# The last chunk of a batch as 128 partitions of seven rows and 64 of one, instead of 120 of eight

## The chip, the core and the metric

The kernel runs on one NeuronCore of a Trainium2 chip. A core has five engines that run side by side: TensorE (PE; its weight loads are shown as PEld), VectorE (DVE), ScalarE (ACT), GpSimd (POOL) and SyncE (SP), which here issues every DMA. The DMAs run on 16 DMA engines. On-chip tiles have up to 128 partitions. The metric is the time of one execution on the device in microseconds; lower is better.

## The reference

Four batches of attention over columns, then a soft mixture of experts over all 20,224 rows of the result:

```python
B, N, C = (4, 5056, 256)
qn = q / (np.linalg.norm(q, axis=1, keepdims=True) + 1e-06)
kn = k / (np.linalg.norm(k, axis=1, keepdims=True) + 1e-06)
s = kn.transpose(0, 2, 1) @ qn / tau          # 256 x 256 a batch, summed over N rows
a = softmax(s)                                # over the last axis
x = (v @ a).reshape(B * N, C)
logits = x @ phi                              # 32 slots
d = softmax(logits, axis=0)                   # over all 20,224 rows
slot_input = d.T @ x
slot_out[e] = np.maximum(slot_input[e] @ w1[e], 0) @ w2[e]     # 8 experts, 4 slots each
c = softmax(logits, axis=1)
out = c @ slot_out
```

All data are float32.

## The kernel before

The 5,056 rows of a batch are cut into chunks of 1,024 rows. In a chunk each of the 128 partitions holds eight rows (J = 8) that follow each other in memory, 1 KB a row. Four chunks take 4,096 rows; 960 are left, and the fifth and last chunk is laid out as 120 partitions of eight:

```python
while t0 < N:
    pc = min(P, (N - t0) // J)
    chunks.append((t0, pc))
    t0 += pc * J
```

Everything that touches a chunk works on `:pc` partitions, so on 120 of them for the last chunk of each batch. Rows may stand on any partition, as the sums over rows don't depend on their order, and the softmax over slots is by row; only the store has to put each row back in its place.

**Scores.** `load_qk` loads q and k in halves of four rows a partition into a tile `raw` (five buffers; L135 for q, L136 for k: 512 KB each, 480 KB in the last chunk). `scores_chunk` makes a rounded copy and a remainder of some of the rows (`hl`: the cast on ScalarE, L160; the difference on VectorE, L161), squares for the norms (ScalarE, L164; added up on VectorE, L188 to L194), and the scores `S` on TensorE (L179). `attention` (L202 to L267) turns the scores of a batch into a matrix M; it takes a power on GpSimd (L218).

**Slots.** `load_v` loads v chunk by chunk (six buffers, L144). `turn_v` transposes a chunk on TensorE (`vTp`, L288) and copies it out (`vT`, L295 and L293). `logits_chunk` makes the logits `L` (L313): the 1,024 columns of a chunk stand as four groups of 32 partitions, and where the last chunk has fewer, a memset fills in −1e30 (L309). `gather_chunk` sums weighted rows of v into `G` (L401), after which the buffer of that v chunk is free.

**Experts and output.** The weights come as 1 MB tiles (L551, L554). At the end, for each chunk, TensorE forms the output from `soh` and `sol` (L733, L734), ScalarE and VectorE copy it out of PSUM (L737, L739) into a tile `o`, and a DMA stores it (L746, L748: 1 MB a chunk, 960 KB for the last of a batch).

**Order.** The order of SP's DMAs is that of the program text: the loads of q and k run ahead, v chunks between them. Each of them waits for its buffer to be free, and for one of eight semaphores that the DMAs take in turn, so that at most eight are on their way. What waits on SP holds up all DMAs behind it. On the other engines a scheduler sets the order up to the last batch; from there TensorE's order too is that of the text. Each engine then works through its order in turn.

Of the kernel before, what the change touches and what calls it, by code (L numbers as in the profile page):

```python
# [17 lines left out]
def colnorm_attention_soft_moe(  # L18
# [29 lines left out]
    PRE = 2  # L48
    NF = F // P
    HF = 4  # L50
    chunks = []
    t0 = 0
    while t0 < N:
        pc = min(P, (N - t0) // J)
        chunks.append((t0, pc))
        t0 += pc * J
    NCH = len(chunks)
    NT = NCH * J

    const = ctx.enter_context(tc.tile_pool(name="const", bufs=1))  # L60
# [47 lines left out]
    mend = keep.tile([P, 1], F32, name="mend")  # L108
    groups = [[(0, 3), (3, NCH)]] * B

    def rows(t, b, ch):
        t0, pc = chunks[ch]
        return t[b, t0 : t0 + pc * J, :].rearrange("(p j) c -> p j c", j=J)

    NS = 3

# [5 lines left out]
    ctx.enter_context(tc.manual_schedule(engines={mybir.EngineType.SP}))  # L122
    st = [dict() for _ in range(B)]

    def half_rows(t, b, ch, h):
        t0, pc = chunks[ch]
        t0 += h * pc * HJ
        return t[b, t0 : t0 + pc * HJ, :].rearrange("(p j) c -> p j c", j=HJ)

    def load_qk(b, ch):  # L130
        pc = chunks[ch][1]
        r = []
        for h in range(2):
            raw = apool.tile([P, 2, HJ, C], F32, tag="raw", name=f"raw{b}_{ch}_{h}", bufs=5)
            nc.sync.dma_start(raw[:pc, 0], half_rows(q, b, ch, h))  # L135
            nc.sync.dma_start(raw[:pc, 1], half_rows(k, b, ch, h))  # L136
            r.append(raw)
        st[b]["raw", ch] = r

    def load_v(b, ch, vt=None):  # L140
        pc = chunks[ch][1]
        if vt is None:
            vt = vpool.tile([P, J, C], F32, tag="v", name=f"v{b}_{ch}")
        nc.sync.dma_start(vt[:pc], rows(v, b, ch))  # L144
        st[b]["v", ch] = vt

    def scores_chunk(b, ch):
# [150 lines left out]
    def logits_chunk(b, ch):  # L298
        pc = chunks[ch][1]
        M = st[b]["M"]  # L300
        lo, hi = [g for g in groups[b] if g[0] <= ch < g[1]][0]
        if ch == lo:
            st[b]["mx", lo] = bpool.tile([P, 3], F32, tag="mxs", name=f"mxs{b}_{ch}", bufs=2)
            st[b]["lt", lo] = bpool.tile([P, 3, J, S], F32, tag="lt", name=f"lt{b}_{ch}", bufs=2)
        lt, mxs = st[b]["lt", lo], st[b]["mx", lo]
        L = pb.tile([P, 2, J, S], F32, tag="amisc" if b == B - 1 and ch == NCH - 2 else "L", name=f"L{b}_{ch}")[:, 0]
        rem = pc - S * (G - 1)
        if rem < S:
            nc.vector.memset(L[S * (G - 1) :, :, rem:], -1e30)  # L309
        for m in range(2):  # L310
            for g in range(G):
                w = min(S, pc - S * g)
                nc.tensor.matmul(  # L313
                    L[S * g : S * g + S, :, :w],
                    M[:, m, :],
                    st[b]["vT", ch, m][:, :, S * g : S * g + w],
                    start=m == 0,
                    stop=m == 1,
                )
# [391 lines left out]
    for b in range(B):  # L711
        for ch in range(NCH):
# [26 lines left out]
                    ev = nc.vector.tensor_copy(od, op[:pc])  # L739
            if (b, ch) in CE:  # L740
                combine(CE[b, ch], ev, nc.vector)
            r0 = b * N + t0
            dst = out[r0 : r0 + pc * J, :].rearrange("(p j) c -> p j c", j=J)
            if b == 0 and ch == 0:
                for lo, hi in CUT:
                    nc.sync.dma_start(dst[:, lo:hi, :], ot[:pc, lo:hi])  # L746
            else:
                nc.sync.dma_start(dst, ot[:pc])  # L748


_INS = ["q", "k", "v", "tau", "moe_phi", "moe_w1", "moe_w2"]
# [36 lines left out]
```

## Time and profile before

| | |
|---|---|
| median of 3 runs | 344.69 us (343.5 to 347.13) |
| profiled execution | 342.7 us, of which the profile's span is 340.9 |
| mean granted TensorE clock | 0.971 |
| busy: TensorE / weight loads / VectorE / ScalarE / GpSimd | 90% / 70% / 73% / 70% / 3% |
| DMA | 100.04 MB, mean 293 GB/s; read 78.94 MB, written 20.71 MB |
| chain that ended last | TensorE 53%, DMA 13%, VectorE 13%, ScalarE 10% |

The rows of the profile name an engine, a line of the kernel, an operation, and what it writes and reads. A shape such as `120*128` after a matmul gives the rows and columns of TensorE that it uses. "x4" is a count. What stands in brackets, or behind the bar, is how long the engine had been idle just before, and what ended it. "DMA to landing" is the time from the issue of a DMA on SP until all of it has arrived. In the stretches "DMA share" is how busy the 16 DMA engines were, and PEclk the share of TensorE's full clock that was granted.

### The profile page before, as it was taken

The page shows a single profiled execution, that of the slowest core. Times are in us where ns is not written, and L with a number is a line of the kernel's source. Part 1 is how long each engine was busy: PE and PEld are TensorE (multiplying, and loading weights), DVE is VectorE, ACT ScalarE, POOL GpSimd, SP SyncE. Part 2 cuts the span into 40 slices and gives each one's busy share as a digit, 9 for nine tenths or more (in the row PEclk, how much of TensorE's full clock was granted, in tenths as well). Part 3 has the DMA queues.
Part 4 walks back from the last instruction along what each step waited for, and adds up shares of the span by engine and source line. Part 5 has one row for each costly group of instructions (what it writes and reads, how often), then busy time and mean ns, then how long its engine had stood idle before and what let it go on. Part 6 is the DMA issues. An engine that isn't in the chain of part 4 may idle for free.

```text
span 340.9 us, 6200 instructions
## 1 busy us (share of the span) xinstructions
PE 305.3 (90%) x2460; PEld 239.9 (70%) x2460; DVE 250.3 (73%) x410; ACT 237.3 (70%) x306; POOL 11.5 (3%) x16
## 2 busy tenths in 40 slices
PE   3999899979999998999999899998889998989850
PEld 2898788979788877877887675665544575767530
DVE  1788999986789894978799397578968077986440
ACT  3788889966998975889799395554334258795620
POOL 0000001000001000000100000105000000000000
PEclk9999999998999998799999999999999999999995
DMA  6999989998797179999903994999979317999995
GB/s 252 380 388 255 398 304 374 299 316 315 248 324 258 52 214 275 418 370 288 375 14 101 271 318 121 423 294 417 413 272 426 127 60 320 310 412 360 373 404 196
DMA packets 20244, 100.04 MB, mean 293 GB/s; under 512 B 2744, under 2 KB 2744, under 8 KB 13240
## 3 DMA queue, kind: packets, MB, share of 16 engines
q1 hardware_dynamic: 20216, 99.66, 81.9%
q8 instruction: 19, 0.31, 0.4%
q14 instruction: 9, 0.07, 0.1%
HBM read 78.94 MB, written 20.71 MB: 292 GB/s over the span
## 4 chain that ended last, share of the span: by engine, by line
PE 53%; DMA 13%; DVE 13%; ACT 10%; issue 5%; SPq 2%; POOL 0%; DVEq 0%; ACTq 0%
PE S L179 18%; DMA raw<-in_k_dram 8%; PE vTp L288 7%; DMA v<-in_v_dram 5%; PE op L733 5%; PE L L313 4%; ACT sq L164 4%; PE op L734 4%; PE G L401 3%; ACT hl L160 2%; DVE o L739 2%; PE H L648 2%; PE O L674 2%; PE cTp L722 2%; DVE sq L188 1%
## 5 line engine op out<-in xcount | busy, mean ns | idle before, releaser
L179 PE MATMUL S<-hl 128*128 128x256 f32 (+1 forms) x648 | 102.0, 304 | 0.8 <-ACT hl L160 0.4
L179 PEld LDWEIGHTS S<-hl 128*128 128x128 f32 (+1 forms) x648 | 86.5, 197 | 8.6 <-issue 4.1
L164 ACT ACTIVATE sq<-raw 128x2048 f32<-128x2048 f32 (+1 forms) x40 | 76.9, 1922 | 10.7 <-DVE sq L188 4.7
L161 DVE TENSOR_TENSOR hl<-raw,hl 128x1536 fp32r<-128x1536 f32 (+3 forms) x39 | 63.5, 1628 | 18.3 <-ACT hl L160 18.2
L160 ACT CAST hl<-raw 128x1536 fp32r<-128x1536 f32 (+3 forms) x39 | 53.8, 1380 | 21.8 <-DMA raw<-in_k_dram 12.0
L179 PE MATMUL S<-raw 128*128 128x256 f32 (+1 forms) x208 | 55.9, 403 | 9.5 <-DMA raw<-in_k_dram 7.8
L188 DVE TENSOR_TENSOR sq<-sq,sq 128x2048 f32<-128x2048 f32 (+1 forms) x20 | 45.8, 2288 | 7.7 <-ACT sq L164 7.3
L179 PEld LDWEIGHTS S<-raw 128*128 128x128 f32 (+1 forms) x208 | 39.3, 204 | 14.5 <-issue 8.2
L288 PE MATMUL vTp<-ident,v 128*128 128x128 f32 (+1 forms) x320 | 42.7, 275 | 3.0 <-DMA v<-in_v_dram 2.9
L295 ACT COPY vT<-vTp 128x512 f32<-128x512 f32 (+1 forms) x70 | 39.2, 589 | 8.2 <-PE vTp L288 7.3
L288 PEld LDWEIGHTS vTp<-ident,v 128*128 128x128 f32 (+1 forms) x320 | 35.3, 142 | 9.5 <-issue 6.8
L733 PE MATMUL op<-soh,cT 128*128 128x512 f32 (+1 forms) x80 | 34.1, 426 | 4.5 <-ACT o L737 2.3
L737 ACT COPY o<-op 128x1024 f32<-128x1024 f32 (+1 forms) x26 | 26.4, 1023 | 10.1 <-PE op L734 10.1
L734 PE MATMUL op<-sol,cT 128*128 128x512 f32 (+1 forms) x80 | 31.6, 395 | 0.0
L739 DVE COPY o<-op 128x1024 f32<-128x1024 f32 (+1 forms) x14 | 17.1, 1223 | 13.0 <-PE op L734 13.0
L313 PE MATMUL L<-vT,M 128*32 128x256 f32 (+1 forms) x320 | 22.8, 383 | 1.7 <-DVE cm L570 1.5
L189 DVE TENSOR_TENSOR sq<-sq 128x1024 f32<-128x1024 f32 (+1 forms) x20 | 24.3, 1213 | 0.0
L733 PEld LDWEIGHTS op<-soh,cT 128*128 128x128 f32 (+1 forms) x80 | 14.9, 186 | 12.7 <-DVE o L739 5.7
L401 PE MATMUL G<-v,dn 128*32 128x256 f32 (+1 forms) x320 | 20.0, 382 | 0.5 <-DVE zacc L389 0.5
L727 ACT CAST cT<-cTp 128x512 fp32r<-128x512 f32 (+1 forms) x20 | 11.7, 589 | 10.3 <-PE cTp L722 5.3
L734 PEld LDWEIGHTS op<-sol,cT 128*128 128x128 f32 (+1 forms) x80 | 15.0, 187 | 2.4
L401 PEld LDWEIGHTS G<-v,dn 128*32 128x32 f32 (+1 forms) x320 | 9.8, 109 | 7.0 <-ACT gs L430 1.0
(122 smaller groups left out, 285.4 us busy)
## 6 DMA issues: line engine op xcount, KB each, us to landing
raw<-in_q_dram SPq DMA_DIRECT2D x32, 512.0 KB, 7.4
raw<-in_k_dram SPq DMA_DIRECT2D x32, 512.0 KB, 8.1
v<-in_v_dram SPq DMA_DIRECT2D x16, 1024.0 KB, 8.7
w<-in_moe_w_dram SPq DMA_DIRECT2D x16, 1024.0 KB, 15.7
out_dram<-o SPq DMA_DIRECT2D x15, 1024.0 KB, 6.6
raw<-in_q_dram SPq DMA_DIRECT2D x8, 480.0 KB, 8.4
raw<-in_k_dram SPq DMA_DIRECT2D x8, 480.0 KB, 10.1
v<-in_v_dram SPq DMA_DIRECT2D x4, 960.0 KB, 15.6
```

The lines of the kernel that those rows point to most:

```text
L160: nc.scalar.copy(hl[:pc, 0, :, :ns], raw[:pc, :, :ns])
L161: nc.vector.tensor_tensor(hl[:pc, 1, :, :ns], raw[:pc, :, :ns], hl[:pc, 0, :, :ns].bitcast(F32), op=ALU.subtract)
L164: nc.scalar.activation(sq[:pc], raw[:pc], AF.Square)
L179: nc.tensor.matmul(sps[:, m, :], lhs, rhs, start=first and y == 0 and m == 0, stop=last and y == len(pairs) - 1, skip_group_check=True,)
L188: nc.vector.tensor_tensor(s0[:pc], s0[:pc], s1[:pc], op=ALU.add)
L288: nc.tensor.transpose(tp[:, jj, :pc], vt[:pc, 4 * hh + jj, P * m : P * m + P], ident[:pc, :pc])
L295: nc.scalar.copy(dst, tp[:, :, :pc])
L313: nc.tensor.matmul(L[S * g : S * g + S, :, :w], M[:, m, :], st[b]["vT", ch, m][:, :, S * g : S * g + w], start=m == 0, stop=m == 1,)
L401: nc.tensor.matmul(gp[S * g : S * g + S, :], dn[ch - lo][:pc, j, :], vt[:pc, j, :], start=ch == lo and j < G, stop=ch == hi - 1 and j >= G,)
L733: nc.tensor.matmul(dst, cT[:, 2 * hh + jj, :pc], soh, start=True, stop=False)
L734: nc.tensor.matmul(dst, cT[:, 2 * hh + jj, :pc], sol, start=False, stop=True)
L737: nc.scalar.copy(od, op[:pc])
```

## The change

The last chunk now uses all 128 partitions. Its 960 rows are 128 partitions of seven rows (896 rows) and 64 partitions that have one row more; the eighth row of the other 64 partitions (`TL` = 64 and up) doesn't exist. A generator `pieces` yields, for each load or store of a chunk, one part or, where the eighth row is in it, two. So for the last chunk the second halves of q and k are two DMAs each (128 partitions of 3 KB, 64 of 1 KB), v is two (128 of 7 KB, 64 of 1 KB), and the store is two. That is 16 DMAs more. The missing eighth row is filled with zeros in q, k and v by memsets on GpSimd, and with −1e30 in the logits by VectorE. All other operations on the last chunk work on 128 partitions, or on 256 and 224 columns in the logits where they had three times 256 and once 192.

```diff
-    chunks = []
-    t0 = 0
-    while t0 < N:
-        pc = min(P, (N - t0) // J)
-        chunks.append((t0, pc))
-        t0 += pc * J
-    NCH = len(chunks)
+    NCH = -(-N // (P * J))
+    chunks = [(P * J * ch, P) for ch in range(NCH)]
+    JL = (N - chunks[-1][0]) // P
+    TL = N - chunks[-1][0] - P * JL
...
+    def pieces(rows, ch, j0, j1):
+        t0 = chunks[ch][0]
+        jm = min(j1, JL) if ch == NCH - 1 else j1
+        lo = t0 + P * j0
+        yield slice(0, P), slice(j0, jm), rows[lo : lo + P * (jm - j0), :].rearrange("(p j) c -> p j c", j=jm - j0)
+        if jm < j1:
+            lo = t0 + P * JL
+            yield slice(0, TL), slice(JL, J), rows[lo : lo + TL, :].rearrange("(p j) c -> p j c", j=1)
...
     def load_qk(b, ch):
-        pc = chunks[ch][1]
         r = []
         for h in range(2):
             raw = apool.tile([P, 2, HJ, C], F32, tag="raw", name=f"raw{b}_{ch}_{h}", bufs=5)
-            nc.sync.dma_start(raw[:pc, 0], half_rows(q, b, ch, h))
-            nc.sync.dma_start(raw[:pc, 1], half_rows(k, b, ch, h))
+            if ch == NCH - 1 and h == 1:
+                nc.gpsimd.memset(raw[TL:, :, HJ - 1, :], 0.0)
+            for x, t in enumerate((q, k)):
+                for ps, js, src in pieces(t[b], ch, HJ * h, HJ * h + HJ):
+                    nc.sync.dma_start(raw[ps, x, js.start - HJ * h : js.stop - HJ * h, :], src)
             r.append(raw)
...
-        nc.sync.dma_start(vt[:pc], rows(v, b, ch))
+        if ch == NCH - 1:
+            nc.gpsimd.memset(vt[TL:, JL, :], 0.0)
+        for ps, js, src in pieces(v[b], ch, 0, J):
+            nc.sync.dma_start(vt[ps, js, :], src)
...
-        rem = pc - S * (G - 1)
-        if rem < S:
-            nc.vector.memset(L[S * (G - 1) :, :, rem:], -1e30)
+        if ch == NCH - 1:
+            nc.vector.memset(L[TL:, JL, :], -1e30)
         for m in range(2):
             for g in range(G):
-                w = min(S, pc - S * g)
+                je = JL if ch == NCH - 1 and S * g >= TL else J
                 nc.tensor.matmul(
-                    L[S * g : S * g + S, :, :w],
+                    L[S * g : S * g + S, :je, :],
                     M[:, m, :],
-                    st[b]["vT", ch, m][:, :, S * g : S * g + w],
+                    st[b]["vT", ch, m][:, :je, S * g : S * g + S],
...
-            r0 = b * N + t0
-            dst = out[r0 : r0 + pc * J, :].rearrange("(p j) c -> p j c", j=J)
...
             else:
-                nc.sync.dma_start(dst, ot[:pc])
+                for ps, js, dst in pieces(out[b * N : b * N + N, :], ch, 0, J):
+                    nc.sync.dma_start(dst, ot[ps, js, :])
```

Lines after the new function stand two or three further down than before (L179 is now L182, L401 is L403, L748 is L750).

On SP, at the loads of the last chunk of batch 2 (`raw_4_0` and `raw_4_1` are its two halves, `v_1` and `v_2` chunks of batch 1), before:

```order
L144 DMA v_1_220<-in_v_dram 128x2048
L135 DMA raw_4_0_222<-in_q_dram 120x1024
L136 DMA raw_4_0_222<-in_k_dram 120x1024
L135 DMA raw_4_1_225<-in_q_dram 120x1024
L136 DMA raw_4_1_225<-in_k_dram 120x1024
L144 DMA v_2_228<-in_v_dram 128x2048
```

and now:

```order
L147 DMA v_1_228<-in_v_dram 128x2048
L136 DMA raw_4_0_230<-in_q_dram 128x1024
L136 DMA raw_4_0_230<-in_k_dram 128x1024
L136 DMA raw_4_1_233<-in_q_dram 128x768
L136 DMA raw_4_1_233<-in_q_dram 64x256
L136 DMA raw_4_1_233<-in_k_dram 128x768
L136 DMA raw_4_1_233<-in_k_dram 64x256
L147 DMA v_2_239<-in_v_dram 128x2048
```

The first half is one DMA for q and one for k, as before, but of 128 partitions; the second is two for each. The order of the tiles is the same.

On POOL, from the first power (`rn`, one for each batch) on, the number behind a tile's name being its batch, before:

```order
L218 TENSOR_TENSOR rn0_504<-rn0_504,half_88 128x4
L218 TENSOR_TENSOR rn1_902<-rn1_902,half_88 128x4
L218 TENSOR_TENSOR rn2_1508<-rn2_1508,half_88 128x4
L700 MEMSET sol_2913 128x512
L218 TENSOR_TENSOR rn3_2243<-rn3_2243,half_88 128x4
```

and now:

```order
L133 MEMSET raw0_4_1_151 64x2x256
L221 TENSOR_TENSOR rn0_520<-rn0_520,half_88 128x4
L133 MEMSET raw1_4_1_188 64x2x256
L145 MEMSET v0_4_210 64x256
L221 TENSOR_TENSOR rn1_918<-rn1_918,half_88 128x4
L133 MEMSET raw2_4_1_233 64x2x256
L145 MEMSET v1_4_256 64x256
L221 TENSOR_TENSOR rn2_1524<-rn2_1524,half_88 128x4
L133 MEMSET raw3_4_1_279 64x2x256
L145 MEMSET v2_4_2192 64x256
L145 MEMSET v3_4_2204 64x256
```

Behind these follow the memset of `sol` and the power of batch 3, as before. Each power now has one to three memsets ahead of it, which wait until the buffer that they fill is free.

On TensorE, among the scores of batch 3 (`S`, here of its chunk 3) stand the gathers `G_0` of batch 1, whose end frees the v buffers that SP waits for ahead of the last chunk's halves; before:

```order
L288 MATMUL vTp_0_1_1_1941<-ident,v_0_253 128x128 x4
L179 MATMUL S_1630<-hl_3_0_1962 128x256 x4
L401 MATMUL G_0_1603<-v_0_212,dn_0_1597 32x256 x8
L401 MATMUL G_0_1603<-v_1_220,dn_0_1597 32x256 x8
L401 MATMUL G_0_1603<-v_2_228,dn_0_1597 32x256 x8
```

and now:

```order
L291 MATMUL vTp_0_1_1_1957<-ident,v_0_266 128x128 x4
L182 MATMUL S_1646<-raw_3_0_268 128x256 x2
L182 MATMUL S_1646<-hl_3_0_1978 128x256 x11
L403 MATMUL G_0_1619<-v_0_220,dn_0_1613 32x256 x3
L254 MATMUL aTp_1547<-ident,a_1537 128x128 x2
L403 MATMUL G_0_1619<-v_0_220,dn_0_1613 32x256
L254 MATMUL aTp_1547<-ident,a_1537 128x128 x2
L403 MATMUL G_0_1619<-v_0_220,dn_0_1613 32x256 x4
L403 MATMUL G_0_1619<-v_1_228,dn_0_1613 32x256 x8
L403 MATMUL G_0_1619<-v_2_239,dn_0_1613 32x256 x8
```

The gathers moved behind more of the scores and between the transposes `aTp`; the count of TensorE that SP waits for is 1046 for the first of the v chunks, and was 1035. The same gathers in batch 2 have moved by less: the count there is 641, and was 642.

More of the change, by code (lines that the diff above doesn't have):

```diff
@@ L50, in colnorm_attention_soft_moe @@
     HF = 4
-    chunks = []
-    t0 = 0
-    while t0 < N:
-        pc = min(P, (N - t0) // J)
-        chunks.append((t0, pc))
-        t0 += pc * J
-    NCH = len(chunks)
+    NCH = -(-N // (P * J))
+    chunks = [(P * J * ch, P) for ch in range(NCH)]
+    JL = (N - chunks[-1][0]) // P
+    TL = N - chunks[-1][0] - P * JL
+    assert JL == J - 1 and TL % S == 0 and 0 < TL < P
     NT = NCH * J
@@ L109, in colnorm_attention_soft_moe @@
     groups = [[(0, 3), (3, NCH)]] * B
-    def rows(t, b, ch):
-        t0, pc = chunks[ch]
-        return t[b, t0 : t0 + pc * J, :].rearrange("(p j) c -> p j c", j=J)
+    def pieces(rows, ch, j0, j1):
[6 more added lines that the diff above has]
+            yield slice(0, TL), slice(JL, J), rows[lo : lo + TL, :].rearrange("(p j) c -> p j c", j=1)
     NS = 3
@@ L123, in colnorm_attention_soft_moe @@
     st = [dict() for _ in range(B)]
[L125 to L128, printed above, removed]
     def load_qk(b, ch):
-        pc = chunks[ch][1]
         r = []
@@ L741, in colnorm_attention_soft_moe @@
                 combine(CE[b, ch], ev, nc.vector)
-            r0 = b * N + t0
-            dst = out[r0 : r0 + pc * J, :].rearrange("(p j) c -> p j c", j=J)
             if b == 0 and ch == 0:
+                dst = out[: P * J, :].rearrange("(p j) c -> p j c", j=J)
                 for lo, hi in CUT:
-                    nc.sync.dma_start(dst[:, lo:hi, :], ot[:pc, lo:hi])
+                    nc.sync.dma_start(dst[:, lo:hi, :], ot[:, lo:hi])
             else:
-                nc.sync.dma_start(dst, ot[:pc])
+                for ps, js, dst in pieces(out[b * N : b * N + N, :], ch, 0, J):
+                    nc.sync.dma_start(dst, ot[ps, js, :])
 _INS = ["q", "k", "v", "tau", "moe_phi", "moe_w1", "moe_w2"]
```

## The prediction

> **What bounds the kernel now.** I read the page first, then the stretches, then the rows where TensorE stands still.
>
> ```profile
> span 340.9 us, 6200 instructions
> ...
> PEclk9999999998999998799999999999999999999995
> ...
> PE 53%; DMA 13%; DVE 13%; ACT 10%; issue 5%; SPq 2%; POOL 0%; DVEq 0%; ACTq 0%
> PE S L179 18%; DMA raw<-in_k_dram 8%; PE vTp L288 7%; DMA v<-in_v_dram 5%; PE op L733 5%; PE L L313 4%; ACT sq L164 4%; PE op L734 4%; PE G L401 3%; ACT hl L160 2%; DVE o L739 2%; PE H L648 2%; PE O L674 2%; PE cTp L722 2%; DVE sq L188 1%
> ```
>
> The chain that ended last is TensorE work for 53%; for 13% it is a wait for loads of k and v. The clock row is nearly all nines, with an 8 and a 7 inside the run. So TensorE is the bound, and what can be won there is the time in which it waits for a load, and the half clock that follows. Whether the changed transfers are behind this, the stretches tell:
>
> ```profile
> core 0: us, PE busy (x) PEld busy (x) DVE busy (x) ACT busy (x) POOL busy (x), PEclk, DMA share, GB/s
> 14.10:24.30 10.20, 10.20 (x68) 9.56 (x67) 9.29 (x9) 8.33 (x7) 0.00 (x0) 1.00 1.03 412
> 26.20:34.80 8.60, 8.26 (x54) 7.50 (x54) 7.75 (x7) 6.78 (x5) 0.00 (x0) 1.00 1.01 264
> 75.50:78.90 3.40, 3.40 (x17) 3.22 (x16) 0.00 (x0) 0.63 (x1) 0.00 (x0) 0.50 0.94 359
> 133.50:140.30 6.80, 6.68 (x27) 5.99 (x27) 6.80 (x9) 6.38 (x8) 0.00 (x0) 0.50 0.98 379
> 326.30:333.70 7.40, 2.78 (x11) 1.56 (x9) 2.45 (x2) 1.07 (x2) 0.00 (x0) 0.85 1.01 421
> ```
>
> In the first stretch only q and k halves of 128 partitions land, in the second mainly those of 120 partitions (batch 0, last chunk). The DMA engines are full in both (share 1.0), but move 412 GB/s in one and 264 in the other. A half of 512 KB (524,288 bytes) thus costs 524,288 / 412,000 = 1.27 us of the queue, a 120-partition half of 480 KB 491,520 / 264,000 = 1.86 us, though it is smaller. The same in batch 2, seen at its landings:
>
> ```profile
> 120.82 0.33 SPq L144 DMA_DIRECT2D v<-in_v_dram  x1
> 121.25 0.39 SPq L135 DMA_DIRECT2D raw<-in_q_dram  x1
> 121.69 0.40 SPq L136 DMA_DIRECT2D raw<-in_k_dram  x1
> ```
>
> ```profile
> v<-in_v_dram SPq DMA_DIRECT2D x1, 1024.0 KB, 4.9
> raw<-in_q_dram SPq DMA_DIRECT2D x2, 480.0 KB, 9.1
> raw<-in_k_dram SPq DMA_DIRECT2D x2, 480.0 KB, 11.3
> ```
>
> The v chunk lands at 120.82 + 4.9 = 125.7. Where TensorE waits, below, the first k half of 120 partitions has just landed, at 131.5: two such halves took 5.8 us, 2.9 each. I take 1.86 and 2.9 as the bounds of one, and 2.2 as the value, nearer the stretch, in which the queue is never empty.
>
> ```profile
> 64.55 9.74 DMA v<-in_v_dram
> ```
>
> ```profile
> 74.42 0.63 PE L288 MATMUL vTp<-ident,v 128*128 128x128 f32 x4 [2.16 <-DMA v<-in_v_dram]
> ...
> 131.62 1.10 PE L179 MATMUL S<-raw 120*128 120x256 f32 x4 [1.17 <-DMA raw<-in_k_dram]
> ...
> 194.65 1.10 PE L179 MATMUL S<-raw 120*128 120x256 f32 x4 [1.18 <-DMA raw<-in_k_dram]
> 196.14 0.38 PE L179 MATMUL S<-hl 120*128 120x256 f32 x1 [0.39 <-ACT hl L160]
> ```
>
> These are TensorE's longest waits for loads after the start: site A at 74.4 (a v chunk queued behind batch 1's four 120-partition halves), B at 131.6 and C at 194.7 (the 120-partition halves of batches 2 and 3 themselves). A and B stand just ahead of the two stretches at clock 0.50, C is followed by none.
>
> **The change, part by part.** Sums are against the profiled execution, 342.7 us (span 340.9, 1.8 around it); the median of the runs is 344.69, 2.0 more, and I add that at the end.
>
> *Loads.* Per batch, four slow halves (4 × 2.2 = 8.8 us of queue) become two full halves (2 × 1.27), two of 384 KB (393,216 / 412,000 = 0.95) and two pieces of 64 KB. A 64-row transfer is not in the trace. Its bytes alone are 0.16 us; from above it is bounded by what a whole small transfer takes from issue to landing:
>
> ```profile
> out_dram<-o SPq DMA_DIRECT2D x2, 256.0 KB, 2.3
> out_dram<-o SPq DMA_DIRECT2D x1, 512.0 KB, 2.9
> ```
>
> From 256 to 512 KB only 0.6 us are added, so most of the 2.3 is latency, which a full queue overlaps. Nearest is the issue time of a row above, 0.4 us, the pace at which SP can hand such pieces over; I take 0.4, and keep 0.16 and 2.3. New queue time: 2.54 + 1.9 + 0.8 = 5.2 us a batch against 8.8, so 3.6 earlier behind the chunk (2.2 if a slow half is only 1.86), and at B the first k half lands at 125.7 + 2 × 1.27 = 128.3, not 131.5.
>
> - Site A: v needs to be 74.3 − 72.3 = 2.0 us earlier, and comes 3.6 earlier. The wait of 2.16 goes, and with it, if the clock follows the wait, the half clock: 3.4 us full of matmuls at 0.50 lose about 1.6. Gain 3.7. What is late next is ScalarE's cast (L160), which itself waited for TensorE there.
> - Site B: k is there at 128.3, before TensorE arrives at 130.45 (131.62 − 1.17). Gain 1.17, plus up to half of 6.68 us of matmuls at 0.50; I take 3.0. Gain 4.2.
> - Site C: the waits are 1.18 + 0.39 = 1.6. But the rows moved here: the gather matmuls of batch 1 stand further back among the scores of batch 3, and SP, which waits for them before it issues a v chunk and behind it the last halves of batch 3, waits for a count of TensorE that is 11 higher. Eleven score matmuls are
>
> ```profile
> 186.20 1.55 PE L179 MATMUL S<-hl 128*128 128x256 f32 x11
> ```
>
> 1.5 us. The first k half comes 2 × (1.86 − 1.27) = 1.2 to 3.3 us sooner behind its v chunk, and that chunk 1.5 later: they about cancel. Gain 0.1, between −0.3 and 1.6.
> - Batch 0: VectorE and ScalarE carry the chain there; I count nothing.
>
> [...]
>
> *Stores.* In the last part VectorE paces the chunks:
>
> ```profile
> 327.04 1.24 DVE o L739
> ...
> 329.62 1.23 DVE o L739
> ```
>
> 2.58 us each; the queue moves a full chunk at 421 GB/s in 1,048,576 / 421,000 = 2.49. Queue and pace nearly match, so each slow store leaves a backlog:
>
> ```profile
> out_dram<-o SPq DMA_DIRECT2D x3, 1024.0 KB, 3.9
> ```
>
> ```profile
> out_dram<-o SPq DMA_DIRECT2D x1, 960.0 KB, 9.0
> ```
>
> The first three full stores land 3.9 us after their issue, the last store, the kernel's end, 9.0 after. With two parts (917,504 / 421,000 = 2.18, and 0.4) a batch's five chunks take 4 × 2.49 + 2.6 = 12.6 us of queue against 12.9 us of pace: no backlog grows. The last store then lands 3.9 + 0.4 (second issue) = 4.3 after: gain 4.7, I take 4.5. With 2.3 for the piece, 14.4 against 12.9 leaves 1.5 a batch, and the gain is gone.
>
> *Added work.* Transposes of v see 128 columns for 120:
>
> ```profile
> L288 PE MATMUL vTp<-ident,v 128*128 128x128 f32 x256 | 34.6, 276 | 3.0 <-DMA v<-in_v_dram 2.9
> ...
> L288 PE MATMUL vTp<-ident,v 120*128 120x120 f32 x64 | 8.3, 270 | 0.0
> ```
>
> 64 × 6 ns = 0.4 us, on the bound. The logits keep their columns (two of 256 and two of 224, for three of 256 and one of 192). The eight memsets on POOL are each at most
>
> ```profile
> L699 POOL MEMSET soh<- 128x512 f32 x1 | 0.5, 524 | 6.4 <-DVE vT L293 6.4
> ...
> POOL rn L218 <- DVE rn L217: 161.2, 3, 54.9
> ```
>
> 0.5 us, and are covered: POOL sits idle for 161 us in three stretches ahead of the power (L218) that every batch's softmax needs. They stand ahead of that power in POOL's order, but wait for readers of buffers that SP also waits for before the same chunk's load, long before the power. If that cover failed, softmax and all behind it would wait. The casts and first scores of the last half now wait for memset and load; the load is longer. Sixteen more issues at 0.4 us on SP fall where SP waits for buffers anyway.
>
> Sum: 3.7 + 4.2 + 0.1 + 4.5 − 0.4 = 12.1; 342.7 − 12.1 = 330.6, and 2.0 to the median: **332.6 us**.
>
> **Rivals.**
> 1. *Only the end is won.* TensorE's waits at A and B are taken over by casts and by SP, which waits for the gathers before it loads, and the half clock shows up elsewhere. For it: ScalarE and VectorE are busy for most of these stages; the clock's dips are two events in one execution. Against it: at B both were idle for the load. It gives 342.7 − 4.5 + 0.4 = 338.6, 340.6 at the median's level.
> 2. *The transfers don't get faster:* the low rate comes from the place in memory or from what runs beside. Against it: loads and stores of 120 partitions both are slow, full chunks ahead and behind aren't. It gives 344.7 ± 1. [...]
> 3. *Slower: the pieces of 64 rows are full-price transfers.* If one takes over (8.8 − 4.4) / 2 = 2.2 us of the queue, the last chunk lands later than now, and that decides. At the 2.3 of the 256 KB row it is about break-even. At the 2.9 of the 512 KB row the halves are 2 × 0.7 = 1.4 us later, at A, B and C together 4.2, less the 1.2 that the first k half still wins at B; the stores leave 4 × 2.49 + 2.18 + 2.9 − 12.9 = 2.1 a batch, 8.6 in all, where they leave 9.0 − 3.9 = 5.1 now, 3.5 more. That is 342.7 + 3.0 + 3.5 + 0.4 = 349.6, with 2.0 351.6. Against it: halves that follow each other land at 1.27 us, so a transfer's own latency is not paid in the queue. [...]
>
> **How the numbers follow.** Forecast (327 to 336) 0.62, the first rival (337 to 341) 0.18, the second 0.12, the third 0.08. The low end takes C in full (1.6), B's full half clock (3.4) and the slow halves at 2.9: 327.5. The range goes from there through the first rival, which leaves out some 0.2: **327.5 to 341**. About 1% (3.4 us) is what a measurement here can tell from no change: faster, below 341.2, gets the forecast and most of the first rival, 0.79; same 0.14; slower 0.07.
>
> **What would show it.** Right: the stretches in which batches 0 to 3 load their last chunks move about 400 GB/s; TensorE's row at the first v transpose of chunk 2 (A) and at the last halves (B, C) has no wait for a load; the clock row has nines where the 8 and the 7 stood; the last store lands some 4 us after its issue. Wrong: transfers of 64 rows that land 2 us or more behind their neighbours, a power on POOL that starts behind a memset, or half-clock stretches of 3.4 us that only moved.

## The result, and the profile after

| | before | changed |
|---|---|---|
| median, same chip | 345.91 us (4 runs, 343.5 to 348.1) | 333.12 us (4 runs, 331.1 to 336.4) |
| ratio | 1 | 0.961, 95% interval 0.951 to 0.972 |
| profiled execution, span | 342.7, 340.9 us | 331.1, 328.9 us |
| mean granted clock | 0.971 | 0.987 |

The change saves 12.8 us in the medians, 11.6 in the profiled executions. The ratios, here and below, leave out as slow each run that is over 1.5% above the fastest of its kernel; the medians hold all runs. The page after, in the lines that stood first in the prediction:

```profile
span 328.9 us, 6253 instructions
...
PEclk9999999999999999999999999999997999999997
...
PE 60%; DVE 13%; ACT 11%; issue 6%; DMA 6%; SPq 1%; POOL 1%; DVEq 0%; ACTq 0%; POOLq 0%
PE S L182 20%; PE vTp L291 8%; PE op L735 5%; ACT sq L167 5%; PE G L403 4%; PE L L315 4%; PE op L736 4%; DMA raw<-in_k_dram 4%; PE H L650 3%; DVE o L741 2%; PE O L676 2%; PE cTp L724 2%; DMA v<-in_v_dram 2%; DVE sq L191 2%; ACT hl L163 2%
```

The chain waits for loads of k and v for 6% where it was 13%. The two 8s and the 7 inside the clock row are gone, but a 7 has come at slice 31, among the experts. The stretches, the first with 128-partition halves as before, the next two in which the last chunks of batches 2 and 3 land:

```profile
core 0: us, PE busy (x) PEld busy (x) DVE busy (x) ACT busy (x) POOL busy (x), PEclk, DMA share, GB/s
14.10:24.30 10.20, 10.16 (x66) 9.24 (x65) 9.30 (x9) 8.39 (x7) 0.52 (x1) 1.00 1.03 412
...
122.70:129.70 7.00, 7.00 (x52) 6.05 (x50) 3.77 (x7) 5.28 (x4) 0.00 (x0) 1.00 1.04 375
184.20:189.80 5.60, 5.60 (x52) 4.52 (x51) 4.87 (x5) 3.02 (x3) 0.00 (x0) 1.00 1.05 374
```

A last chunk now loads at about 375 GB/s, and TensorE is busy for every microsecond of both stretches. TensorE's rows at the three sites (the bracket is the wait and what ended it):

```profile
72.96 0.63 PE L291 MATMUL vTp<-ident,v 128*128 128x128 f32 x4 [1.01 <-DMA v<-in_v_dram]
...
127.77 1.03 PE L182 MATMUL S<-raw 128*128 128x256 f32 x4
...
188.23 1.03 PE L182 MATMUL S<-raw 128*128 128x256 f32 x4
```

The first half of the last chunk has no bracket any more at B and C. A still has one, of 1.01 us. The last store of the program, its two parts and the time from issue to landing:

```profile
out_dram<-o SPq DMA_DIRECT2D x1, 896.0 KB, 3.8
out_dram<-o SPq DMA_DIRECT2D x1, 64.0 KB, 3.6
```

That was 9.0. Cut at the starts of the four copies of the finished scores on ScalarE (`ssb<-S`, L213, L210 before) and at the last copy of `o`, two traces of the changed kernel (the second is an experiment below) stand against before like this, in us:

| stretch | before | changed | changed, again |
|---|---|---|---|
| scores of batch 0 | 41.8 | 42.3 | 42.4 |
| batch 1 (site A) | 45.8 | 42.7 | 44.2 |
| batch 2 (site B) | 57.2 | 53.0 | 53.1 |
| batch 3 (site C) | 61.7 | 60.2 | 61.9 |
| from there to the last copy of `o` | 123.1 | 124.4 | 122.7 |
| from there to the last landing | 11.3 | 6.3 | 6.3 |
| span | 340.9 | 328.9 | 330.6 |

Two rows repeat to 0.1 us: site B (−4.1) and the end (−5.0). Sites A and C and the experts differ by 1.5 to 1.7 us between two executions of the same program, so one trace doesn't size them.

### The profile page after: what moved, and what is told of

It is laid out like the page before. It is cut to its first block, busy times and chain, and to the rows that moved or that the text cites. A ratio compares the mean times of both kernels' runs of the same rounds, so it can differ in the third digit from the quotient of the medians.

```text
span 328.9 us, 6253 instructions
## 1 busy us (share of the span) xinstructions
PE 302.8 (92%) x2460; PEld 236.5 (72%) x2460; DVE 249.7 (76%) x410; ACT 237.1 (72%) x306; POOL 14.7 (4%) x24
## 4 chain that ended last, share of the span: by engine, by line
PE 60%; DVE 13%; ACT 11%; issue 6%; DMA 6%; SPq 1%; POOL 1%; DVEq 0%; ACTq 0%; POOLq 0%
PE S L182 20%; PE vTp L291 8%; PE op L735 5%; ACT sq L167 5%; PE G L403 4%; PE L L315 4%; PE op L736 4%; DMA raw<-in_k_dram 4%; PE H L650 3%; DVE o L741 2%; PE O L676 2%; PE cTp L724 2%; DMA v<-in_v_dram 2%; DVE sq L191 2%; ACT hl L163 2%
## 5 line engine op out<-in xcount | busy, mean ns | idle before, releaser
L182 PE MATMUL S<-hl 128*128 128x256 f32 x648 | 98.9, 298 | 0.7 <-DVE hl L164 0.7
L182 PEld LDWEIGHTS S<-hl 128*128 128x128 f32 x648 | 83.7, 190 | 8.3 <-issue 4.5
L167 ACT ACTIVATE sq<-raw 128x2048 f32<-128x2048 f32 x40 | 77.0, 1924 | 11.2 <-DVE sq L191 6.0
L164 DVE TENSOR_TENSOR hl<-raw,hl 128x1536 fp32r<-128x1536 f32 (+1 forms) x39 | 63.5, 1627 | 8.0 <-ACT hl L163 8.0
L163 ACT CAST hl<-raw 128x1536 fp32r<-128x1536 f32 (+1 forms) x39 | 53.9, 1382 | 14.0 <-DMA raw<-in_k_dram 8.5
L182 PE MATMUL S<-raw 128*128 128x256 f32 x208 | 53.9, 392 | 7.3 <-DMA raw<-in_k_dram 5.7
L191 DVE TENSOR_TENSOR sq<-sq,sq 128x2048 f32<-128x2048 f32 x20 | 45.8, 2288 | 7.3 <-ACT sq L167 7.1
L182 PEld LDWEIGHTS S<-raw 128*128 128x128 f32 x208 | 38.0, 197 | 11.6 <-issue 5.6
L291 PE MATMUL vTp<-ident,v 128*128 128x128 f32 x320 | 43.5, 277 | 1.8 <-DMA v<-in_v_dram 1.0
L298 ACT COPY vT<-vTp 128x512 f32<-128x512 f32 x70 | 39.2, 597 | 6.1 <-PE vTp L291 5.5
L735 PEld LDWEIGHTS op<-soh,cT 128*128 128x128 f32 x80 | 15.0, 187 | 12.5 <-DVE o L741 5.6
L403 PE MATMUL G<-v,dn 128*32 128x256 f32 x320 | 20.8, 382 | 0.5 <-DVE zacc L391 0.5
L403 PEld LDWEIGHTS G<-v,dn 128*32 128x32 f32 x320 | 9.9, 109 | 7.1 <-ACT gs L432 1.0
```

Source lines behind the costliest of these rows:

```text
L163: nc.scalar.copy(hl[:pc, 0, :, :ns], raw[:pc, :, :ns])
L164: nc.vector.tensor_tensor(hl[:pc, 1, :, :ns], raw[:pc, :, :ns], hl[:pc, 0, :, :ns].bitcast(F32), op=ALU.subtract)
L167: nc.scalar.activation(sq[:pc], raw[:pc], AF.Square)
L182: nc.tensor.matmul(sps[:, m, :], lhs, rhs, start=first and y == 0 and m == 0, stop=last and y == len(pairs) - 1, skip_group_check=True,)
L191: nc.vector.tensor_tensor(s0[:pc], s0[:pc], s1[:pc], op=ALU.add)
L291: nc.tensor.transpose(tp[:, jj, :pc], vt[:pc, 4 * hh + jj, P * m : P * m + P], ident[:pc, :pc])
```

## The experiments

The kernels were timed on three chips, on each beside the kernel before. Two of the ratios' bases are thin: that of q and k only rests on two of its six runs, and on the third chip (the last three rows) before scattered from 337.6 to 350.9 us and only three of its twelve runs count. So the ratio of the medians stands beside, and kernels on the third chip are compared by their medians.

| kernel | median us (runs) | before, same chip | ratio, 95% | of medians |
|---|---|---|---|---|
| q and k only | 341.35 (6) | 343.76 | 0.975, 0.967 to 0.983 | 0.993 |
| v and stores only | 339.21 (6) | 343.76 | 0.989, 0.984 to 0.995 | 0.987 |
| old stores | 337.10 (6) | 343.76 | 0.979, 0.973 to 0.986 | 0.981 |
| old q, k in batch 2 | 334.78 (6) | 346.25 | 0.965, 0.958 to 0.971 | 0.967 |
| pieces in four | 331.97 (6) | 346.25 | 0.960, 0.955 to 0.966 | 0.959 |
| v ahead | 333.88 (6) | 346.25 | 0.965, 0.960 to 0.971 | 0.964 |
| old q, k in batch 1 | 334.90 (6) | 344.34 | 0.984, 0.977 to 0.992 | 0.973 |
| old q, k in batch 3 | 335.76 (6) | 344.34 | 0.987, 0.979 to 0.996 | 0.975 |
| changed, again | 332.53 (6) | 344.34 | 0.979, 0.971 to 0.987 | 0.966 |

### Transfers by themselves

Only DMAs, in groups: `dma_start(t[:rows, :j], q[...])`, eight back to back into eight buffers (four at 8 KB a row), for several numbers of rows and of KB a row.

> Transfers alone: the attention and the experts are left out, and what is stored is a constant. Groups of eight loads back to back (four in the groups with 8 KB a partition), each group started after the one before has landed: 128, 120, 112, 96 and 64 partitions of 4 KB, 124 and 60 partitions of 4 KB, 128 of 3 KB, 128 of 3 KB and 64 of 1 KB in turn, 64 of 1 KB alone, 128 and 120 of 8 KB; then four stores each of 128 and of 120 partitions of 8 KB, and of 128 of 7 KB with 64 of 1 KB. My theory, a 120-partition transfer is slow by its shape: 128x4 KB at about 410 GB/s (1.27 us each), 120x4 KB at about 264 (1.86 us each), stores of 120x8 KB slower by the same factor than 128x8 KB, and a 64-row piece adds 0.2 to 0.45 us to the 384 KB beside it. [...] Rival, the shape is innocent and the place in memory or the neighbours make the last chunk slow: 120x4 KB runs at 385 to 410 GB/s here. Rival of the full-price piece: pairs take 2 us each and more over the 384 KB alone.

The stretches lie inside the groups, where the queue is full: loads of 128, 120, 112, 96, 64, 124 and 60 partitions of 4 KB, then of 128 of 3 KB, and of 128 and 120 of 8 KB; the last two are stores of 128 and 120 partitions of 8 KB. The last two columns are the DMA share and GB/s.

```profile
3.00:11.00 8.00, 0.00 (x0) 0.00 (x0) 1.00 0.97 371
18.00:30.00 12.00, 0.00 (x0) 0.00 (x0) 1.00 0.96 241
36.50:46.00 9.50, 0.00 (x0) 0.00 (x0) 1.00 1.03 268
52.50:60.00 7.50, 0.00 (x0) 0.00 (x0) 1.00 1.03 253
68.00:73.00 5.00, 0.00 (x0) 0.00 (x0) 1.00 1.03 208
85.00:115.00 30.00, 0.00 (x0) 0.00 (x0) 1.00 0.26 105
122.00:128.00 6.00, 0.00 (x0) 0.00 (x0) 1.00 0.97 197
134.50:139.50 5.00, 0.00 (x0) 0.00 (x0) 1.00 0.97 341
...
185.00:191.00 6.00, 0.00 (x0) 0.00 (x0) 1.00 1.01 426
197.00:206.00 9.00, 0.00 (x0) 0.00 (x0) 1.00 0.95 218
227.00:233.00 6.00, 3.59 (x3) 0.00 (x0) 1.00 1.02 423
240.00:249.00 9.00, 3.43 (x2) 0.00 (x0) 1.00 0.91 342
```

The shape alone does it: 120 partitions move 241 GB/s where 128 move 371, and 218 against 426 at 8 KB, with no compute beside them and at another place in memory. That is the end of the second rival. Nor is it that 120 rows can't be shared out evenly among 16 engines: 112 and 96 can, and are nearly as slow (268 and 253), with the engines full (share 1.03). The same 384 KB load at 341 GB/s as 128 rows of 3 KB and at 253 as 96 rows of 4 KB. 124 partitions fall to 105 GB/s with a DMA share of 0.26, as much as four engines of sixteen. Stores of 120, four in a row, lose less (342 against 423); in two parts, 128 of 7 KB and 64 of 1 KB, they move 373. The pairs of 384 KB and 64 KB can't be read here, since in this kernel each piece overwrote rows of the transfer ahead of it and waited for it.

### Halves of the partitions

The same with other rows: `t[64:128]`, low and high halves in turn, 64 and 56 for 120, and a 64 KB piece in a column of its own.

> Transfers alone again, in groups that start when the one before has landed; attention and experts are left out, and one chunk of zeros is stored. Loads of 4 KB a partition: 128 partitions, the lower 64, the upper 64, lower and upper 64 in turn, and 120 as 64 and 56; 128 of 3 KB with 64 of 1 KB beside it, and 128 of 3 KB alone; of 8 KB: 128, the lower 64, the lower 32, 128 of 7 KB with 64 of 1 KB, and 120. [...] Theory 2, a DMA of fewer rows is slower for its shape, wherever the rows lie: lower, upper and in turn all 208. Theory 3, the descriptors decide (4 KB against 8 KB): 64 and 32 of 8 KB move about 400. For the piece of 64 rows of 1 KB beside 128 of 3 KB: my prediction has 0.4 us for it; the rival of the full price has 2.2 and more.

In this order: 128, the lower 64, the upper 64, both in turn; 128 of 3 KB with the piece, and without; the lower 64 and the lower 32 of 8 KB.

```profile
3.00:11.00 8.00, 0.00 (x0) 0.00 (x0) 1.00 0.98 374
17.00:25.00 8.00, 0.00 (x0) 0.00 (x0) 1.00 0.99 208
29.50:37.50 8.00, 0.00 (x0) 0.00 (x0) 1.00 1.02 205
41.50:49.00 7.50, 0.00 (x0) 0.00 (x0) 1.00 1.03 231
...
62.00:67.00 5.00, 0.00 (x0) 0.00 (x0) 1.00 0.91 279
71.50:75.00 3.50, 0.00 (x0) 0.00 (x0) 1.00 0.86 313
...
90.00:107.00 17.00, 0.45 (x4) 0.00 (x0) 1.00 1.02 208
112.50:119.50 7.00, 0.00 (x0) 0.00 (x0) 1.00 1.02 206
```

Half of the partitions move 205 to 208 GB/s of 374, wherever they lie, and a quarter moves as much as a half (206 and 208): the rate doesn't go with the number of partitions, by which 32 would have moved 208 / 2 = 104, and Theory 3 fails at its 400. Theory 2 fits, but only says that anything short of 128 is slow. The piece can be priced: 384 KB alone take 393,216 / 313,000 = 1.26 us, with 64 KB beside them 458,752 / 279,000 = 1.64. That is 0.4 us for a piece. 120 partitions cut into 64 and 56 move 214, no more than whole. The v load of the change, 128 of 7 KB with 64 of 1 KB, moves 373, where 128 of 8 KB move 417 and 120 of 8 KB 212.

### q and k only

```diff
-            nc.sync.dma_start(vt[ps, js, :], src)
+        nc.sync.dma_start(vt[:pc], rows(v, b, ch))
```

and the logits and the store as before the change.

> Only q and k in the new layout; v, its logits and the store stay at 120 partitions. My theory, the three sites are q's and k's alone: the end of the scores of batch 3 comes as early as in the changed kernel (about 198 us, 8 us sooner than before), the last store still lands 9 us after its issue, and the time is about 338 us (ratio to before 0.978). Rival, v's share matters (a 120-partition v chunk keeps the halves behind it late): 341 us, ratio 0.986. Rival, only the end is won: ratio 1.0.

TensorE's order is here, matmul for matmul, that of the kernel before, so what this trace wins in the scores is won by q and k alone. B and C are won: TensorE has no wait of more than 0.3 us between 100 and 205 us, and batch 2 takes 53.3 us, batch 3 59.4. Site A isn't, although its loads are those of the changed kernel, and the last store is later still than before:

```profile
74.76 0.91 PE L301 MATMUL vTp<-ident,v 128*128 128x128 f32 x4 [2.24 <-DMA v<-in_v_dram]
```

```profile
out_dram<-o SPq DMA_DIRECT2D x1, 960.0 KB, 12.2
```

So new halves don't win site A in every execution: A came out as before, with half clock behind it. The 338 us of the theory were missed too. The scores of batch 3 are done at 201.0 us, 5.5 sooner than before, but of that the trace loses 1.7 among the experts, with 3.4 us at half clock, and 3.2 at the end, where the backlog of slow stores grew. The median of 341.35 is the first rival's number; its reason, halves kept late by v, isn't what B and C show. The runs spread from 333.5 us at a mean clock of 0.990 to 344.3 at 0.968.

### v and stores only

The reverse: `raw[:120]` in halves of 120 partitions, the rest as changed.

> The reverse: q and k stay in halves of 120 partitions, v, logits and stores are in the new layout. My theory: the waits at the three sites and the half clock behind them stay (scores of batch 3 end at about 206 us), the last store lands about 4 us after its issue, and the time is 5 us shorter than before (ratio 0.986, 341 us). If the two halves of the change add up, this ratio and that of q and k alone multiply to the 0.961 of the whole. Rival, only the end is won: the same 0.986, but q and k alone then give 1.0. Rival, the stores win nothing by their shape: ratio 1.0.

```profile
65.70:69.10 3.40, 3.08 (x15) 3.12 (x16) 2.67 (x3) 1.70 (x3) 0.00 (x0) 0.50 0.99 264
```

```profile
131.52 1.10 PE L186 MATMUL S<-raw 120*128 120x256 f32 x4 [0.34 <-DMA raw<-in_k_dram]
...
193.82 1.10 PE L186 MATMUL S<-raw 120*128 120x256 f32 x4 [0.75 <-DMA raw<-in_k_dram]
```

The waits for k are back, the half clock stands at 65.7 (TensorE waits 2.29 us for v there), and batch 3 ends at 205.2. The last store lands 3.8 us after its issue. The ratio is near the 0.986 expected. That the two halves of the change add up is shown by the traces in the main: q and k alone end the scores 5.5 us sooner, v and stores alone shorten the end by 5.0, together 10.5 of the 12.0 us. The times leave it open: the ratios multiply to 0.989 × 0.975 = 0.964, near the whole 0.961, but those of the medians to 0.993 × 0.987 = 0.980. That only the end is won is refuted by the trace of q and k alone.

### Old stores

```diff
-                for ps, js, dst in pieces(...):
-                    nc.sync.dma_start(dst, ot[ps, js, :])
+                nc.sync.dma_start(dst, ot[:120])
```

> The changed kernel, but the store of the last chunk of each batch is one DMA of 120 partitions again (the rows of the last chunks then land in other places than they belong, and the shape and bytes of the transfer are those of before). My theory, the backlog of the stores alone makes the end late: the last store lands about 9 us after its issue, and the time is 4.5 to 5 us over the changed kernel (ratio to before 0.975, about 337 us). Rival, the end came earlier because the engines ahead of it did, and a slow store is hidden: same as the changed kernel, ratio 0.961.

The first row is the end of the old-stores kernel, the second the stretch of before in which its first store of 120 partitions lands:

```profile
out_dram<-o SPq DMA_DIRECT2D x1, 960.0 KB, 8.2
```

```profile
292.80:298.00 5.20, 5.20 (x26) 3.88 (x25) 4.53 (x7) 2.92 (x5) 0.00 (x0) 1.00 0.93 262
```

The last store is late again, the way from the last copy to the last landing takes 10.4 us where it took 6.3, and the time is 4.6 us over the changed kernel (337.1 against the 332.5 of its second timing, below, on another chip), as expected. TensorE's order is that of the changed kernel. In the trace of before, the four stores of 120 partitions land 5.3, 3.1, 4.3 and 2.8 us behind the store ahead of them, most full ones 2.5.

### One site undone at a time

```diff
+            if b == 2:          # 1 or 3 in the two others
+                nc.sync.dma_start(raw[:120, 0], half_rows(q, b, ch, h))
+                nc.sync.dma_start(raw[:120, 1], half_rows(k, b, ch, h))
```

> The changed kernel, with q and k of batch 2's last chunk alone back in halves of 120 partitions (v, logits, stores and the other batches stay new). My theory, site B is won by the transfers of that batch alone: TensorE again waits about 1.2 us for k near 130 us, half clock follows, and the time is 4.2 us over the changed kernel (ratio to before 0.973). If the half clock at B was chance and only the wait belongs to the transfers: 1.2 us over it (0.965). Rival, site B was won by something else (the order of the gathers, v): no wait for k there and 0.961.

> The changed kernel, with q and k of batch 1's last chunk alone back in halves of 120 partitions: site A undone. My prediction's price of site A, 3.7 us with its half clock: ratio to before 0.972. Theory from the runs so far, site A is a narrow race that the new layout wins only in some executions (TensorE waited 1.0 us there in the changed kernel, 2.2 and 2.3 us in two kernels with the same loads of batch 1, with half clock behind it): undoing it costs less, 1 to 2 us in the median, ratio 0.964 to 0.967. Rival, A has nothing to do with the layout: 0.961.

> The changed kernel, with q and k of batch 3's last chunk alone back in halves of 120 partitions: site C undone. My prediction had 0.1 us for C, since the gathers moved: ratio as the changed kernel, 0.961. What the two traces showed, 1.5 us shorter scores in batch 3: TensorE waits for k again near 189 us, 1.2 to 1.6 us, ratio 0.966.

The kernels in that order, each with its waits:

```profile
74.61 0.63 PE L302 MATMUL vTp<-ident,v 128*128 128x128 f32 x4 [2.29 <-DMA v<-in_v_dram]
131.53 1.13 PE L193 MATMUL S<-raw 120*128 120x256 f32 x4 [0.67 <-DMA raw<-in_k_dram]
134.83 2.29 PE L193 MATMUL S<-hl 120*128 120x256 f32 x17 [0.65 <-DVE hl L175]
```

```profile
75.10 0.63 PE L302 MATMUL vTp<-ident,v 128*128 128x128 f32 x4 [3.32 <-DMA v<-in_v_dram]
```

```profile
74.32 0.63 PE L302 MATMUL vTp<-ident,v 128*128 128x128 f32 x4 [2.01 <-DMA v<-in_v_dram]
...
191.49 1.10 PE L193 MATMUL S<-raw 120*128 120x256 f32 x4 [1.22 <-DMA raw<-in_k_dram]
```

TensorE's order is that of the changed kernel in the first two, and but for six matmuls in the third. Undoing B or C brings back the wait of that site and not the other's; A waits in all three, longest where its own halves are old. In the medians A costs 334.90 − 332.53 = 2.4 us, C 335.76 − 332.53 = 3.2, more than either answer of its expectation, and B some 2.3 (334.78 against the 332.5 of the changed kernel, on another chip). As the six runs of a kernel spread over 3 to 6 us, each of these is uncertain by a microsecond or two. With the stores (4.6) they sum to 12.5 us, near the whole, but that is partly chance, as C's share is worth less against before (see Site C below).

B lies between the two answers of its expectation. Its trace has 1.3 us of waiting at B and no half clock there, and batch 2 takes 55.9 us, 2.9 over the changed kernel. But the runs go with the clock: the two at a mean of 0.994 take 331.6 and 332.6 us, no more than the changed kernel, the four at 0.986 to 0.988 take 334.2 to 335.9, and the profiled one of these has its half clock at A and among the experts.

### The changed kernel again

> The changed kernel as it is, timed beside the two, for a closer ratio and a second trace: ratio 0.961. If site A is a narrow race, the wait of TensorE at the first transposes of chunk 2 (1.0 us in the first trace) differs in this one by a microsecond or more, with nothing changed.

```profile
74.61 0.63 PE L291 MATMUL vTp<-ident,v 128*128 128x128 f32 x4 [2.23 <-DMA v<-in_v_dram]
```

Nothing was changed, and the wait at A is 2.23 us where it was 1.01. The last full k part ahead of it landed at 70.16 in the first trace and 69.80 in this one (72.03 before), but the v chunk behind it at 72.82 and at 74.48 (74.29 before). In the packet records of four traces with a wait of 2.0 us and more behind the new halves (this one, q and k only, and B and C undone) one or two 8 KB packets of this v chunk start at 70.1 to 70.6 us and take 1.2 to 1.9 us, where the median is 0.31; where the wait was 1.01 (the first trace) or 0.30 (old stores), none that starts after 70 us takes over 0.8. That the chunk lands late by this packet fits the times, but no run sets it apart. What holds it up is open. Site C is a close race as well: the first k half landed 1.5 us ahead of TensorE in the first trace, and only 0.1 us ahead in this one (190.12 against 190.25), where TensorE then waits for ScalarE's cast and VectorE's difference of that half:

```profile
191.74 0.38 PE L182 MATMUL S<-hl 128*128 128x256 f32 x1 [0.39 <-ACT hl L163]
...
193.53 2.29 PE L182 MATMUL S<-hl 128*128 128x256 f32 x17 [0.52 <-DVE hl L164]
```

Half clock did not follow at A this time. In the clock records of before and of the changed kernel's first trace the shortest half-clock stretch is 3.413 us long, and the entries stand whole multiples of that apart (19, 1, 16, 2 and 56 in before; 70, 1 and 21 in the changed kernel). So I counted in steps of 3.413 us from a change of the clock in the same trace, and took the steps around A: this kernel, then the one with batch 2 undone.

```profile
70.00:73.40 3.40, 2.38 (x17) 2.03 (x16) 3.40 (x4) 3.04 (x3) 0.00 (x0) 1.00 0.99 381
73.40:76.80 3.40, 2.19 (x19) 2.22 (x20) 2.49 (x4) 1.35 (x2) 0.00 (x0) 1.00 0.79 249
76.80:80.20 3.40, 3.40 (x28) 3.29 (x28) 1.38 (x1) 2.88 (x2) 0.00 (x0) 1.00 1.03 383
```

```profile
72.15:75.55 3.40, 1.11 (x10) 0.96 (x9) 3.40 (x5) 2.55 (x3) 0.00 (x0) 1.00 0.82 306
75.60:79.00 3.40, 3.40 (x17) 3.31 (x16) 0.37 (x1) 0.44 (x1) 0.00 (x0) 0.50 0.93 339
```

A wait of 2.2 to 2.3 us falls across two steps in the one, each busy for over 2 us, and into one step in the other, busy for 1.11: only there the next step is at 0.50, so TensorE needn't stand idle for a whole step to have half clock behind it. In before and in the changed kernel's first trace, each step after the start that was busy for at most 0.42 of its length has half clock behind it (before: 0.37 at A and 0.35 at the end of the work; changed: 0.42 there), and so have the steps with the wait for v in q and k only (0.34), v and stores only (0.42) and batch 2 undone (0.33). Three cases don't follow this count and are not explained: the half clock of before at B (the step ahead of it busy for 0.66), that of the kernel with v ahead at the same place (0.63), and that among the experts (0.90). The last stands in eight of the ten traces with the new layout or part of it; in this one, in the one with pieces in four and in before, the same step, as busy, has none behind it.

### Pieces in four

```diff
-            yield slice(0, TL), slice(JL, J), rows[lo : lo + TL, :]...
+            for p0 in range(0, TL, TL // 4):
+                yield slice(p0, p0 + TL // 4), slice(JL, J), rows[...]
```

> The changed kernel with every piece of 64 rows cut into four DMAs of 16 rows: 48 DMAs more, the bytes the same. By my price (a piece costs the queue what SP needs to issue it, 0.4 us): a last chunk costs SP and queue some 1.2 us more for each of its pieces, 3.6 us for q, k and v, which takes away what the loads won at sites A, B and C, and the last store lands 1.2 us later: 4 to 9 us over the changed kernel (ratio to before 0.973 to 0.987). If extra DMAs are free beside a full queue (SP runs ahead of it): 1 us over it at the end, ratio 0.964. If each of them has a full price of 2 us: 24 us for the loads of a batch, far slower than before (ratio over 1.05).

331.97 us, as the changed kernel, with 48 DMAs more; the end is 0.8 us longer (7.1 us from the last copy to the last landing where it was 6.3). At B and C the last k piece lands at 129.6 and 191.1, as in the changed kernel's traces (129.7 and 131.3; 189.8 and 193.1): behind a full queue the additional DMAs are free. At A they are not. SP needs 0.4 us for each piece there (1.7 for one of them) while the queue runs dry (the last two columns are the DMA share and GB/s); it issues the v chunk at 71.31 us where the changed kernel issued it at 66.58, and the chunk lands at 76.15, not at 72.82 or 74.48:

```profile
68.00:69.00 1.00, 1.00 (x8) 0.92 (x7) 1.00 (x1) 1.00 (x1) 0.00 (x0) 1.00 0.28 60
69.00:70.00 1.00, 1.00 (x9) 0.90 (x8) 0.86 (x2) 1.00 (x5) 0.00 (x0) 1.00 0.10 25
```

```profile
76.53 0.60 PE L292 MATMUL vTp<-ident,v 128*128 128x128 f32 x4
```

TensorE didn't wait for it, because the scheduler has put the first transposes of that chunk 22 matmuls further back, to 76.53. So the 0.4 us of SP that was expected is paid where the queue is empty, and this kernel's order hides it. The rival of full-price pieces is far off.

### v ahead

```diff
+        if i == 2 * NCH - 1:
+            load_v(*early.pop(0))      # ahead of load_qk, behind it in all other steps
         load_qk(i // NCH, i % NCH)
```

> The changed kernel with one DMA in another place: at site A the v chunk (chunk 2 of batch 0) is issued ahead of batch 1's last halves of q and k, where it stood behind them. If the 1.0 us that TensorE still waits there is the place in the queue: v lands some 2.5 us earlier, the wait goes, and the time is 1 us under the changed kernel (ratio to before 0.958). Rival, the scheduler uses the earlier v for earlier transposes (in the order of TensorE the first four of chunk 2 now stand 20 matmuls further ahead) and the wait only moves: same as the changed kernel, within 2 us, 0.961.

```profile
131.72 2.82 PE L291 MATMUL vTp<-ident,v 128*128 128x128 f32 x12 [1.78 <-DMA v<-in_v_dram]
```

The wait at 74 is gone, one of 0.93 for v stands at 65.3, and the one above, of 1.78, at B, with half clock from 131.2. 333.88 us: the rival was right, the wait only moved. It is no test of the one DMA, since the scheduler moved about a quarter of TensorE's matmuls (batch 2 takes 63.4 us, batch 3 53.5). No version that ran is measurably faster than the changed kernel.

## Why the prediction was right, and where it wasn't

The forecast was 332.6 us, the time is 333.1; the sum of 12.1 us stands against 11.6 in the profiled executions. The sum held better than its terms, and that is luck: in the first trace the sites and the stores give 3.1 + 4.2 + 1.5 + 5.0 = 13.8, and 0.5 in batch 0 and 1.3 among the experts, which nobody forecast, take it back to 12.0; in the second A and C give 1.4 together, and the span is 10.3 shorter.

| term | predicted | traces of the whole change | undone alone |
|---|---|---|---|
| A | 3.7 | 1.5 to 3.1 | 2.4 |
| B | 4.2 | 4.1 to 4.2 | 2.3 |
| C | 0.1 | −0.2 to 1.5 | 3.2 |
| stores | 4.5 | 5.0 | 4.6 |

The traces of all kernels together size the sites better than two of them. The time of a batch's scores in us, one figure for each kernel, without pieces in four and v ahead, where TensorE's order at the sites is another:

| scores of | halves of 120 | new halves |
|---|---|---|
| batch 1 (A) | 45.8, 45.6, 46.4 | 42.7, 44.2, 46.0, 42.8, 45.4, 44.1 |
| batch 2 (B) | 57.2 (before, half clock), 55.1, 55.9 | 53.0, 53.1, 53.3, 53.0, 53.0, 52.7 |
| batch 3 (C), order of before | 61.7 | 59.4 |
| batch 3 (C), new order | 61.9, 63.9 | 60.2, 61.9, 61.6, 59.1, 61.4 |

- **The shape as the cause** was right, and is now shown by transfers alone. The two prices were about right: a slow half takes 491,520 / 241,000 = 2.0 us of the queue (2.2 taken), a piece 0.4 (0.4 taken; that it is SP's issue time that is paid shows only at A with pieces in four, where the queue ran dry).
- **Site A** is the step that failed. "The wait of 2.16 goes" doesn't hold: it went to 1.0 in one execution and stayed at 2.2 in the next. The term is mis-sized, 3.7 where the means in the table above differ by 1.7 (45.9 against 44.2), and single executions lie from 0.1 over to 3.2 under the 45.9. The last full k part lands some 2 us sooner (70.16 and 69.80, before 72.03), not 3.6, but 2.0 were needed, and the v chunk behind it landed 1.5 us sooner in one trace and 0.2 later in the other. What is won there is mostly half clock: with waits of 2.01 and 2.23 us that fell into two steps batch 1 took 44.1 and 44.2 us, with waits of 2.24 and 2.29 in one step, and half clock behind them, 46.0 and 45.4.
- **Site B**'s first half was right (no wait for k, in both traces). The 3.0 us of half clock were won against the one trace of before; in the two others with the old halves the waits came back without it, and batch 2 is 2.1 and 2.9 us longer than with the new ones.
- **Site C** came out as forecast: 0.1, between −0.3 and 1.6, against −0.2 and 1.5 in the two traces. So did its two parts. In the order of before the new halves win 61.7 − 59.4 = 2.3 us (1.2 to 3.3 forecast); the new order costs on average 60.8 − 59.4 = 1.4 of it (1.5 forecast): SP issues the first of the v chunks 178.90 − 137.96 = 40.9 us after the end of batch 2's scores, before 183.79 − 144.78 = 39.0, and TensorE comes to the last halves 188.23 − 137.96 = 50.3 us after those scores, before 193.5 − 144.8 = 48.7 (the wait of 1.18 taken off). The 3.2 of C undone is the loads' share in the new order, not what was won against before.
- **The stores** came out as worked out: no backlog, and the last landing 324.27 − 323.88 + 3.6 = 4.0 us after the issue of the last store's first part, where 4.3 was forecast. Batch 0 is 0.5 us longer, where I counted nothing.
- **Added work** costs little, as forecast. The transposes cost 0.6 us (43.5 against 34.6 + 8.3), not 0.4, and the power on POOL still waits for VectorE in batches 0 to 2, not for a memset (that of batch 3 stands behind the memset of `sol`, as before the change):

```profile
L291 PE MATMUL vTp<-ident,v 128*128 128x128 f32 x320 | 43.5, 277 | 1.8 <-DMA v<-in_v_dram 1.0 <-ACT vT L298 0.6
```

```profile
POOL rn L221 <- DVE rn L220: 92.8, 3, 41.6
```

- **"Half clock that only moved"** was named as a sign of being wrong, and came in part. The stretch of 3.4 us among the experts stands in the first trace and in seven others, and that stage takes 124.3 to 126.4 us with it, 122.7 to 123.1 without. But on the whole there is less half clock, and that is no accident of one trace. The mean clock of every run is on record: before's 34 runs have 0.963 to 0.987, the middle one 0.974, the changed kernel's ten 0.983 to 0.994, the middle 0.988 to 0.989. As the clock in the traces is full or half (1.00 or 0.50), that is about 18 us of half clock in 344 and 8 in 333. Of these 9.4 and 4.6 to 4.9 stand at the end of the traces, where TensorE has no work left, so some 9 and 3 us stand in the work. By this estimate 6 us less at half clock are worth up to 3 of the 12.8 us.
- **Two slips in the working.** The clock row of before has two 8s and a 7 inside, not one of each; A has one half-clock stretch, B a longer one. And the low end of 327.5 is 5.1 us under the forecast, of which C in full and B's full half clock are 1.5 and 0.4; what makes the slow halves the other 3.2 isn't said.

## What to carry to other kernels

Lay a chunk that doesn't fill the tile over all 128 partitions with fewer rows each, and give the rest a small DMA of its own: loads of 120, 112 and 96 partitions lost 28 to 49% of the rate, and a small DMA behind others cost about 0.4 us or nothing, but more where the queue ran dry while it was issued. Compare the order of the instructions as well as the times: where an edit lets the scheduler move other work, a time doesn't show the edit alone. A wait that a microsecond decides is no sure gain; take a second trace of the same kernel, or undo that site alone, before its size is believed. Where a wait and half clock stand together, count the half clock at that place as chance: the length of the wait alone didn't settle it here, as waits of 2.16 to 2.29 us for v had half clock behind them in four traces, and one of 2.23 had none. Over all its runs the changed kernel, whose traces have fewer waits, did show less half clock (a mean clock of 0.988 to 0.989 in the middle, against 0.974).

## What the runs showed of the hardware

- A load of 128 partitions of 4 or 8 KB moved 371 to 426 GB/s (of 3 KB 313 to 341), of 120, 112 and 96 partitions 212 to 268, of 64, 60 and 32 from 197 to 208, at a DMA share of 0.95 to 1.03 (0.86 at the 313). 64 and 32 partitions of 8 KB moved the same, 208 and 206. Why shapes short of 128 are slow isn't shown: no run tells which engine writes what.
- 124 partitions moved 105 GB/s at a DMA share of 0.26, as much as 0.26 × 16 = 4.2 engines. Why so little isn't shown.
- The changed kernel's own runs spread from 330.7 to 336.4 us over ten runs; between two of them site A alone differs by 1.5 us.
